# Sums of x ranked behind weight pieces, and first evictions by ScalarE or VectorE, in an attention and mixture-of-experts kernel

## The chip, the cores and the metric

The kernel runs on one core of one Trainium2 chip. The metric is the time of one execution on the device in microseconds (us), the median of several runs. Lower is better. The core's engines are TensorE (PE; PEld is its weight load), VectorE (DVE), ScalarE (ACT), GpSimd (POOL) and SyncE (SP), which issues most transfers. Each engine takes its instructions in the order in which the program lists them.

## The reference

Causal attention with a cumulative decay, then a soft mixture of four experts, then a gated network, all in f32:

```python
cum = np.cumsum(np.maximum(s, 0), axis=-1)
scores = q @ k.T / sqrt(64) + np.minimum(-(cum[:, None] - cum[None, :]), 0)   # causal; 2 x 8 heads, 576 x 64
x = softmax(scores) @ v                                  # heads side by side: x is 1152 x 512
p = domain_probs / domain_probs.sum(-1)                  # 1152 x 4
x = sum(p[:, e:e+1] * (np.maximum(x @ w1[e], 0) @ w2[e]) for e in range(4))    # 512 -> 1024 -> 512
g = x @ w_gate                                           # 512 -> 1536
out = (g / (1 + np.exp(-g)) * (x @ w_val)) @ w_out       # 1152 x 512
```

## The kernel before

**Numbers in two parts.** Every dense operand is split into a high part, rounded to TensorE's f32 format, and a low part, the rest. A product takes three matmuls (high by high, high by low, low by high). Names end accordingly: xh and xl for x, wah and wal for weights that lead in, woh and wol for weights that lead out, hh and hl for the hidden values, wsh and wsl for sums of weights. A high part is a cast, a low part a subtraction.

**Seven products for eight.** Where it pays, a product x @ w is cut in quarters and done with seven products instead of eight, which needs sums of quarters of w (`Weight.halves`, tile sf, line 930) and sums of quarters of x (`sums_of_x`, tile tt, line 1097). A sum of x is some additions and subtractions of two operands in SBUF, then a cast (line 307) and a low part (line 320). The seven results are added up in the tile cc by VectorE straight out of the banks (lines 1177 and 1198).

**Stages.** The 1152 tokens go in two parts, 0 to 512 (four tiles of 128 tokens) and 512 to 1152 (five tiles). A stage leads one part of the tokens through 256 hidden columns. Its matmuls in (tile h) alternate with the matmuls out (tile o) of the stage before. A tile of output is six matmuls into one bank of PSUM, called o. Then it is evicted: `moe1_out` multiplies it by the expert's share p and writes it into acc_a (first part) or acc_b (second part) the first time (line 1302), and adds it to what is there every later time (line 1304). `moe2_out` copies the first time (line 1447) and adds later (line 1449). All evictions are on VectorE. There are three o banks in the dense part, so a tile waits until the tile three before it has been evicted.

**The order.** The program plans itself while it is written. Every task has an engine or a choice of engines with a cost each, the tasks it depends on, and a rank. At each step the task with the earliest start goes next, and among equal starts the one with the lowest rank. A task with a choice takes the engine for which start plus 1.6 times the cost is least, with 1.0 us on top for VectorE in the dense part. Evictions and what else TensorE soon waits for have the rank `prompt()`, 69 at the end of attention. Weight pieces (casts and low parts of a weight, in two pieces each) have 100 plus the number of the weight, and 11 weights are planned by then. The sums of x for the first part had the rank 70, thus behind evictions and ahead of all weight pieces; those for the second part had 109. They are planned when attention ends, near 145 us. The chosen order is fixed in the program: on the chip an engine waits for the next instruction in its list even if a later one could run.

In `COST` a sum of two operands (kind "two") of 256 columns is put at 0.48 us on VectorE and 0.81 us on GpSimd, a read of a bank (kind "bank") of 512 columns at 0.61 us on VectorE and 0.48 us on ScalarE.

Of the kernel before, what the change touches and what calls it, by code (L numbers as in the profile page):

```python
# [55 lines left out]
WRANK = 100  # L56
# [28 lines left out]
def f32(ap):  # L85
    return ap.bitcast(F32)
# [13 lines left out]
def dve(c, n=1):  # L100
    return n * 0.07 + 0.00105 * c
# [11 lines left out]
def choices(engines, kind, c, n=1):  # L113

    return {e: n * COST[kind][e][0] + c * COST[kind][e][1] for e in engines}
# [38 lines left out]
class Plan:  # L154
# [8 lines left out]
    def add(self, eng, cost, run=None, deps=(), take=(), give=(), rank=0.0):  # L163
        t = Task(eng, cost, run, [d for d in deps if d is not None], take, give, rank)
        if not t.missing:
            self.ready.append(t)
        return t
# [96 lines left out]
def attention_moe_swiglu(ctx, tc, q, k, v, s, dp, w1, w2, wg, wv, wo, out):  # L264
    nc = tc.nc
    B, H, S, D = q.shape
    N, DM = out.shape
# [26 lines left out]
    late = {}  # L294
    plan = Plan()
    add = plan.add
    rings = {}

    def ring(name, n=2):
        return rings.setdefault(name, Ring(n))  # L300

    def any_of(engines, kind, c, run, deps, n=1, **kw):
        return add(choices(engines, kind, c, n), None, run, deps, **kw)

    def move(e, to, x):
        if e == "a":
            nc.scalar.copy(to, x)  # L307
        elif e == "v":
            nc.vector.tensor_copy(to, x)
        else:  # L310
            nc.gpsimd.tensor_scalar(to, f32(x), 1.0, 1.0, op0=ALU.mult, op1=ALU.mult)
# [7 lines left out]
    def minus(e, to, x, y):  # L319
        {"v": nc.vector, "p": nc.gpsimd}[e].tensor_tensor(to, x, f32(y), op=ALU.subtract)  # L320
# [10 lines left out]
    def pieces():  # L331

        for (tok, n), pos in zip(runs, place):
            a = 0
            while a < n:
                t, p = divmod(pos + a, P)
                m = min(P - p, n - a)
                yield t, slice(p, p + m), slice(tok + a, tok + a + m)
                a += m
# [636 lines left out]
    def acc(t):  # L976
        if t < HALF // P:
            return acc_a[:, t, :]
        return late["acc"][:, t - HALF // P, :]
# [15 lines left out]
    made = {"n": 0}  # L995
# [40 lines left out]
    def prompt():  # L1036
        return newest["i"] - DRANK

    def needs_x(t0, t1):
        if t0 in x_ready:  # L1040
            return x_ready[t0]
        return [x for g in range(len(groups)) if place[g] < t1 for x in done_x[g]]
# [31 lines left out]
    def sums_of_x(t0):  # L1074

        n = (N - HALF if t0 else HALF) // 2
        box = late["T", t0]

        deps = needs_x(t0, t0 + 2 * n) + late.get("sums", [])
        done = box["done"] = {}  # L1080

        def quarter(x, i, j, c):
            return f32(x[:, 2 * i + c, t0 + j * n:t0 + j * n + n])
        tmp = {}
        rg = ring("tt")

        rank = WRANK + made["n"] - 2 if t0 else prompt() + 1
        SUB, ADD = ALU.subtract, ALU.add

        def total(name, x, y, op, deps, new=False):  # L1090

            def task(c, at):
                def run(on):
                    if new and c == 0:
                        tmp[name] = late["t"].tile([P, 6 * P], F32, name="tt", tag="tt", bufs=2)[:, :2 * n].rearrange("p (c n) -> p c n", c=2)
                    x_, y_ = (tmp[z][:, c] if isinstance(z, str) else quarter(*z, c) for z in (x, y))
                    {"v": nc.vector, "p": nc.gpsimd}[on].tensor_tensor(tmp[name][:, c], x_, y_, op=op)
                return any_of(TADD, "two", n, run, at, take=[rg] if new and c == 0 else [], rank=rank)
            first = task(0, deps[0])
            return [first, task(1, deps[1] + ([first] if new else []))]  # L1100

        def chain(*lists):
            return [[x[c] for x in lists] for c in range(2)]

        def parts(i, name, t):
            done[i] = []
            for c in range(2):
                def high(on, c=c):
                    move(on, box["h"][:, i, c], tmp[name][:, c])

                def low(on, c=c):
                    minus(on, box["l"][:, i, c], tmp[name][:, c], box["h"][:, i, c])
                hi = any_of(THIGH, "copy", n, high, [t[c]], rank=rank)
                done[i].append(any_of(TLOW, "two", n, low, [hi], rank=rank))
            return done[i]
        a1 = total("T1", (xh, 0, 1), (xh, 0, 0), SUB, [deps, deps], True)
        t = total("T1", "T1", (xl, 0, 1), ADD, chain(a1))
        t1 = total("T1", "T1", (xl, 0, 0), SUB, chain(t))
        a2 = total("T2", (xh, 1, 1), "T1", SUB, chain(t1), True)
        t2 = total("T2", "T2", (xl, 1, 1), ADD, chain(a2))  # L1120
        u2 = parts(1, "T2", t2)
        u1 = parts(0, "T1", t1)

        t = total("T1", "T2", (xh, 0, 0), SUB, chain(u1, t2))
        t3 = total("T1", "T1", (xl, 0, 0), SUB, chain(t))
        u3 = parts(2, "T1", t3)
        add(None, 0.0, None, u3, give=[(a1[0], rg)])
        t = total("T2", (xh, 1, 0), "T2", SUB, chain(u2, t3))
        u4 = parts(3, "T2", total("T2", "T2", (xl, 1, 0), ADD, chain(t)))
        add(None, 0.0, None, u4, give=[(a2[0], rg)])  # L1130
        late["sums"] = [x for y in done.values() for x in y]
# [73 lines left out]
    def order(st):  # L1205

        return [t for t in ORDER if st.t0 <= t * P < st.t1]
# [32 lines left out]
    fresh = set(range(NT))  # L1240
    last_acc = {}
# [51 lines left out]
    def moe1_out(w, st, e):  # L1293
        items = []

        for t in order(st):
            def evac(x, taker, bank_, t=t):
                def run():
                    sc = pr[:, t, e:e + 1]
                    if t in fresh:  # L1300
                        fresh.remove(t)
                        nc.vector.tensor_scalar(acc(t), bank_(), sc, None, op0=ALU.mult)
                    else:
                        nc.vector.scalar_tensor_tensor(acc(t), bank_(), sc, acc(t), op0=ALU.mult, op1=ALU.add)  # L1304
                a = add("dve", 0.74, run, [x, last_acc.get(t), late["gates"]], give=[(taker, ring("o"))], rank=prompt())
                last_acc[t] = a
                left[t] -= 1
                if left[t] == 0:
                    turn_x(t, a)
            items += outof(w, st, t, evac)  # L1310
        return items
# [129 lines left out]
    def moe2_out(w, st, first, last):  # L1441
        items = []
        for t in order(st):
            def evac(x, taker, bank_, t=t):
                def run():
                    if first:
                        nc.vector.tensor_copy(acc(t), bank_())  # L1447
                    else:
                        nc.vector.tensor_tensor(acc(t), bank_(), acc(t), op=ALU.add)
                deps = [x, last_acc.get(t)] + (turning[st.t0]["turned"] if first else [])  # L1450
                a = add("dve", dve(DM), run, deps, give=[(taker, ring("o"))], rank=prompt())
                last_acc[t] = a
                if last:
                    for p, tok in [y[1:] for y in pieces() if y[0] == t]:
                        add("dma", (0.65, 0.37) if p.stop - p.start < P else (0.48, 0.73), lambda p=p, tok=tok: nc.sync.dma_start(out[tok, :], acc(t)[p, :]), [a], rank=0)
            items += outof(w, st, t, evac)
        return items
# [124 lines left out]
    with ExitStack() as st:  # L1582
        late["ps"] = st.enter_context(tc.tile_pool(name="psb", bufs=1, space=PSUM, reuse_waits="tile"))
        late["t"] = st.enter_context(tc.tile_pool(name="tm", bufs=2, reuse_waits="tile"))
        late["h"] = late["t"]
        late["acc"] = late["t"].tile([P, NT - HALF // P, DM], F32, name="acc_b", bufs=1)
        for t0, n in ((0, HALF), (HALF, N - HALF)):
            late["T", t0] = {x: late["t"].tile([P, 4, 2, n // 2], F32R, name=f"x{x}{t0}", bufs=1) for x in "hl"}
            sums_of_x(t0)
        late["made_n"] = 0  # L1590
        plan.held = HELD2
        rings["h"].n, rings["o"].n = 5, 3
        feed()
        while plan.step():
            feed()
# [24 lines left out]
```

## Time and profile before

| | us |
|---|---|
| median of 3 runs | 749.46 (749.1 to 751.05) |
| profiled execution | 744.91 |
| its span, first to last instruction | 743.1 |
| TensorE busy in it | 717.8 (97%) |
| VectorE busy | 626.6 (84%) |
| GpSimd busy | 440.2 (59%) |
| ScalarE busy | 362.8 (49%) |

The span is attention up to about 143 us (with dense work filling in from 39 us on), the mixture of experts up to about 528 us, and the gated network. TensorE's granted clock is full all the time. A busy share is a mean over parts with different limits, so the places at which TensorE waits, and what runs on the other engines there, tell more than the shares. The times in the rows are us from the start of the span; "idle before" stands in square brackets, with the instruction that ended it.

### The profile page before, as it was taken

How to read it: one execution, taken by the hardware profiler on the slowest of the kernel's cores; microseconds unless marked ns; L12 is line 12 of the kernel's file. 1: busy time of each engine (PE TensorE's matmuls, PEld its weight loads, DVE VectorE, ACT ScalarE, POOL GpSimd, SP SyncE). 2: the span in 40 equal slices, each digit the busy share in tenths (PEclk: the TensorE clock that was granted, in tenths of full speed). 3: DMA queues.
4: the chain of work that ended last, by engine and by line, in shares of the span. 5: the costliest groups of instructions: out<-in, count | busy, mean ns of one | idle time of the engine just before them, and what ended most of it. 6: DMA issues, size and time to landing. Idle time of an engine off the chain costs nothing. (4 is left out here: it accounts for less than half of the span.)

```text
span 743.1 us, 12433 instructions
## 1 busy us (share of the span) xinstructions
PE 717.8 (97%) x4328; PEld 625.4 (84%) x4328; DVE 626.6 (84%) x1273; ACT 362.8 (49%) x808; POOL 440.2 (59%) x456
## 2 busy tenths in 40 slices
PE   8899999998999999999999999998989999999997
PEld 6577776767889989898998989897888999999996
DVE  7979888599678998989999899898997888787765
ACT  6788767324234546455564554574641423232210
POOL 6546865389336456454555455778885676765321
PEclk9999999999999999999999999999999999999999
DMA  5657630010314524444344543622110101010003
GB/s 130 139 119 201 158 90 30 1 56 30 121 49 143 180 82 165 144 168 143 105 165 141 184 156 105 204 90 99 58 57 29 58 30 57 29 58 1 1 1 127
DMA packets 77230, 72.57 MB, mean 98 GB/s; under 512 B 45976, under 2 KB 56280, under 8 KB 77168
## 3 DMA queue, kind: packets, MB, share of 16 engines
q1 hardware_dynamic: 76112, 71.52, 31.3%
q8 instruction: 34, 0.56, 0.3%
q10 hardware_dynamic: 1056, 0.26, 0.2%
q14 instruction: 28, 0.23, 0.1%
HBM read 59.82 MB, written 11.80 MB: 96 GB/s over the span
## 5 line engine op out<-in xcount | busy, mean ns | idle before, releaser
L1220 PE MATMUL o<-woh,hh 128*128 128x512 f32 x396 | 156.5, 395 | 3.6 <-DVE acc_a L1304 2.0
L1221 PE MATMUL o<-wol,hh 128*128 128x512 f32 x396 | 156.1, 394 | 1.7 <-POOL wol L320 1.7
L1222 PE MATMUL o<-woh,hl 128*128 128x512 f32 x396 | 154.8, 391 | 2.2 <-DVE hl L320 2.2
L1177 DVE TENSOR_TENSOR cc<-cc,h 128x320 f32<-128x320 f32 (+1 forms) x288 | 127.7, 451 | 30.6 <-PE h L1160 26.1
L320 POOL TENSOR_TENSOR wal<-raw,wah 128x512 fp32r<-128x512 f32 (+1 forms) x56 | 68.6, 1236 | 71.4 <-ACT wah L307 70.9
L1158 PE MATMUL h<-xh,wsh 128*128 128x320 f32 (+1 forms) x320 | 95.0, 297 | 0.0
L1160 PE MATMUL h<-xh,wsl 128*128 128x320 f32 (+1 forms) x320 | 95.0, 297 | 0.0
L1159 PE MATMUL h<-xl,wsh 128*128 128x320 f32 (+1 forms) x320 | 94.9, 297 | 0.0
L1222 PEld LDWEIGHTS o<-woh,hl 128*128 128x128 f32 x396 | 74.4, 188 | 19.4 <-DVE hl L320 3.0
L1220 PEld LDWEIGHTS o<-woh,hh 128*128 128x128 f32 x396 | 74.5, 188 | 17.4 <-DVE acc_a L1304 2.5
L1221 PEld LDWEIGHTS o<-wol,hh 128*128 128x128 f32 x396 | 74.5, 188 | 13.2 <-POOL wol L320 2.4
L320 POOL TENSOR_TENSOR wol<-raw,woh 128x512 fp32r<-128x512 f32 x52 | 74.4, 1443 | 15.4 <-ACT woh L307 15.2
L1277 ACT ACTIVATE cc<-cc 128x640 f32<-128x640 f32 (+1 forms) x48 | 33.4, 695 | 93.1 <-DVE cc L1177 93.1
L1158 PE MATMUL h<-xh,wah 128*128 128x256 f32 (+1 forms) x240 | 71.3, 297 | 0.0
L1160 PE MATMUL h<-xh,wal 128*128 128x256 f32 (+1 forms) x240 | 71.1, 296 | 0.0
L1159 PE MATMUL h<-xl,wah 128*128 128x256 f32 (+1 forms) x240 | 71.0, 296 | 0.0
L320 POOL TENSOR_TENSOR hl<-cc,hh 128x512 fp32r<-128x512 f32 (+1 forms) x24 | 33.1, 1379 | 50.4 <-DVE hl L823 24.9
L1158 PEld LDWEIGHTS h<-xh,wsh 128*128 128x128 f32 x320 | 60.4, 189 | 1.6
L1159 PEld LDWEIGHTS h<-xl,wsh 128*128 128x128 f32 x320 | 60.5, 189 | 1.4
L1160 PEld LDWEIGHTS h<-xh,wsl 128*128 128x128 f32 x320 | 60.5, 189 | 0.0
L1304 DVE SCALAR_TENSOR_TENSOR acc_b<-o,pr,acc_b 128x512 f32<-128x512 f32 x75 | 55.8, 746 | 4.8 <-PE o L1222 4.1
L307 ACT CAST hh<-sg 128x512 fp32r<-128x512 f32 (+1 forms) x24 | 16.2, 676 | 85.7 <-DVE sg L1421 43.2
(155 smaller groups left out, 1835.1 us busy)
## 6 DMA issues: line engine op xcount, KB each, us to landing
raw<-in_moe_w SPq DMA_DIRECT2D x40, 512.0 KB
n<-hl SPq DMA_DIRECT2D x36, 256.0 KB
raw<-n SPq DMA_DIRECT2D x18, 512.0 KB
hh<-in_moe_w_gate SPq DMA_DIRECT2D x12, 512.0 KB
hh<-in_moe_w_val SPq DMA_DIRECT2D x12, 512.0 KB
hh<-in_moe_w_out SPq DMA_DIRECT2D x12, 512.0 KB
kr<-in_k SPq DMA_DIRECT2D x24, 128.0 KB
vr<-in_v SPq DMA_DIRECT2D x24, 128.0 KB
```

Source lines behind the costliest of these rows:

```text
L307: nc.scalar.copy(to, x)
L320: {"v": nc.vector, "p": nc.gpsimd}[e].tensor_tensor(to, x, f32(y), op=ALU.subtract)
L1158: nc.tensor.matmul(hp, wh, h, start=c == 0, stop=False)
L1159: nc.tensor.matmul(hp, wh, l, start=False, stop=False)
L1160: nc.tensor.matmul(hp, wl, h, start=False, stop=c == 1)
L1177: nc.vector.tensor_tensor(part(k), part(x), banks[i], op=ALU.add)
L1220: nc.tensor.matmul(op, hh[:, f, ts], wh[:, f, :], start=f == 0, stop=False)
L1221: nc.tensor.matmul(op, hh[:, f, ts], wl[:, f, :], start=False, stop=False)
L1222: nc.tensor.matmul(op, hl[:, f, ts], wh[:, f, :], start=False, stop=f == NF - 1)
L1277: nc.scalar.activation(src()[:, o], src()[:, o], AF.Relu)
L1304: nc.vector.scalar_tensor_tensor(acc(t), bank_(), sc, acc(t), op0=ALU.mult, op1=ALU.add)
```

## The change

Three edits. In `sums_of_x` the rank of the sums of the first part becomes 109 (from 70), and that of the second part 111 (from 109). The first eviction of each tile in `moe1_out` (nine in all) and in `moe2_out` (nine) gets a choice between ScalarE and VectorE, at the cost of a bank read; later evictions stay on VectorE. The words for the change also name score operands that are not filled with zeros; the instructions that fill score operands are the same in both programs.

```diff
-        rank = WRANK + made["n"] - 2 if t0 else prompt() + 1
+        rank = WRANK + made["n"] - (0 if t0 else 2)
...
-                def run():
+                new = t in fresh
+                fresh.discard(t)
+
+                def run(on="v"):
                     sc = pr[:, t, e:e + 1]
-                    if t in fresh:
-                        fresh.remove(t)
+                    if on == "a":
+                        nc.scalar.mul(acc(t), bank_(), sc)
+                    elif new:
                         nc.vector.tensor_scalar(acc(t), bank_(), sc, None, op0=ALU.mult)
...
-                a = add("dve", 0.74, run, [x, last_acc.get(t), late["gates"]], give=[(taker, ring("o"))], rank=prompt())
+
+                a = add(choices("av", "bank", DM) if new else "dve", None if new else 0.74, run,
+                        [x, last_acc.get(t), late["gates"]], give=[(taker, ring("o"))], rank=prompt())
...
-                def run():
+                def run(on="v"):
                     if first:
-                        nc.vector.tensor_copy(acc(t), bank_())
+                        move(on, acc(t), bank_())
...
-                a = add("dve", dve(DM), run, deps, give=[(taker, ring("o"))], rank=prompt())
+                a = add(choices("av", "bank", DM) if first else "dve", None if first else dve(DM), run, deps, give=[(taker, ring("o"))], rank=prompt())
```

On GpSimd, behind the four pieces of wah and wal that run from 144.31 us on in the trace of before, there stood (tt is a sum of x, xl_2260 its low part, woh and wol are pieces of an out-weight):

```order
L1097 TENSOR_TENSOR tt<-tt,xl 128x256
L320 TENSOR_TENSOR xl_2260<-tt,xh_2259 128x256 x2
L1097 TENSOR_TENSOR tt<-tt,xl 128x256
L1097 TENSOR_TENSOR tt<-tt,xh 128x256
L320 TENSOR_TENSOR xl_2260<-tt,xh_2259 128x256
L1097 TENSOR_TENSOR tt<-tt,xl 128x256
L311 TENSOR_SCALAR woh<-raw 128x512
L1097 TENSOR_TENSOR tt<-xh,tt 128x256
L320 TENSOR_TENSOR xl_2260<-tt,xh_2259 128x256 x2
L1097 TENSOR_TENSOR tt<-tt,xl 128x256
L320 TENSOR_TENSOR wol<-raw,woh 128x512
```

and now, on the same engine at the same place:

```order
L311 TENSOR_SCALAR woh<-raw 128x512
L1097 TENSOR_TENSOR tt<-xh,tt 128x256
L320 TENSOR_TENSOR wol<-raw,woh 128x512
L311 TENSOR_SCALAR woh<-raw 128x512
L320 TENSOR_TENSOR xl_2260<-tt,xh_2259 128x256
L320 TENSOR_TENSOR wol<-raw,woh 128x512
L1097 TENSOR_TENSOR tt<-tt,xh 128x256
L1097 TENSOR_TENSOR tt<-tt,xl 128x256
L1097 TENSOR_TENSOR tt<-xh,tt 128x256
L311 TENSOR_SCALAR woh<-raw 128x512
```

The first wol piece moved from the twelfth instruction and later to the third; four of the five low parts of sums that stood here left for VectorE.

On VectorE, ahead of the eviction of the first tile of the out stage that begins at 160.97 us in the trace (the last row here), there stood:

```order
L1097 TENSOR_TENSOR tt<-xh,tt 128x256
L1302 TENSOR_SCALAR acc_a<-o,pr 128x512
L1097 TENSOR_TENSOR tt<-tt,xl 128x256
L1302 TENSOR_SCALAR acc_a<-o,pr 128x512
L320 TENSOR_TENSOR xl_2260<-tt,xh_2259 128x256 x2
L1097 TENSOR_TENSOR tt<-xh 128x320
L1261 SCALAR_TENSOR_TENSOR hl<-h,hh 128x512
L1097 TENSOR_TENSOR tt<-xh 128x320
L1097 TENSOR_TENSOR tt<-tt,xl 128x320 x4
L1304 SCALAR_TENSOR_TENSOR acc_a<-o,pr,acc_a 128x512
```

and now (line 1308 is what was 1304):

```order
L1097 TENSOR_TENSOR tt<-xh,tt 128x256
L320 TENSOR_TENSOR xl_2260<-tt,xh_2259 128x256
L1097 TENSOR_TENSOR tt<-tt,xl 128x256
L320 TENSOR_TENSOR xl_2260<-tt,xh_2259 128x256 x3
L1097 TENSOR_TENSOR tt<-xh 128x320
L1261 SCALAR_TENSOR_TENSOR hl<-h,hh 128x512
L1097 TENSOR_TENSOR tt<-xh 128x320
L1097 TENSOR_TENSOR tt<-tt,xl 128x320 x2
L1308 SCALAR_TENSOR_TENSOR acc_a<-o,pr,acc_a 128x512
```

The two first evictions left for ScalarE, low parts of sums came in, and two of the four additions of the next sums moved behind the eviction.

On VectorE in the first stage of the gated network, from 549.86 us on in the trace (hl<-sf is the low part of a weight sum, hl<-sg one of a hidden value, sg the gated value), there stood:

```order
L320 TENSOR_TENSOR hl<-sf,hl 128x512
L1447 COPY acc_a<-o 128x512
L320 TENSOR_TENSOR hl<-sf,hl 128x512
L1177 TENSOR_TENSOR cc<-cc,h 128x320
L1447 COPY acc_a<-o 128x512
L1421 TENSOR_TENSOR sg<-sg,cc 128x640
L1198 TENSOR_TENSOR cc<-cc,h 128x320
L1447 COPY acc_a<-o 128x512
L1177 TENSOR_TENSOR cc<-cc,h 128x320
L1421 TENSOR_TENSOR sg<-sg,cc 128x640
L1447 COPY acc_a<-o 128x512
```

and now (line 1427 is what was 1421):

```order
L320 TENSOR_TENSOR hl<-sf,hl 128x512 x2
L1177 TENSOR_TENSOR cc<-cc,h 128x320
L1427 TENSOR_TENSOR sg<-sg,cc 128x640
L1198 TENSOR_TENSOR cc<-cc,h 128x320
L320 TENSOR_TENSOR hl<-sg,hh 128x640
L1177 TENSOR_TENSOR cc<-cc,h 128x320
L1427 TENSOR_TENSOR sg<-sg,cc 128x640
L320 TENSOR_TENSOR wsl<-sf,wsh 128x512
L1177 TENSOR_TENSOR cc<-cc,h 128x256
L320 TENSOR_TENSOR hl<-sg,hh 128x640
```

The four copies left for ScalarE; two low parts hl<-sg came in from GpSimd, and behind these rows a low part wsl and two weight sums sf went to GpSimd.

## Rows read from the trace of the kernel before

**Rows 1.** Waits of TensorE over the run: waiter, releaser: us in total, times, longest

```profile
PE h L1158 <- DVE cc L1177: 2.7, 3, 1.9
...
PE o L1220 <- DVE acc_a L1304: 2.0, 1, 2.0
PE o L1221 <- POOL wol L320: 1.7, 1, 1.7
...
PE h L1158 <- DVE cc L1198: 0.8, 1, 0.8
```

**Rows 2.** Timeline of TensorE, 160.9 to 184.2 us: start, duration, engine, line, instruction

```profile
164.25 0.50 PE L1221 MATMUL o<-wol,hh 128*128 128x512 f32 x1 [1.71 <-POOL wol L320]
...
168.98 0.39 PE L1220 MATMUL o<-woh,hh 128*128 128x512 f32 x1
169.20 0.39 PE L1221 MATMUL o<-wol,hh 128*128 128x512 f32 x1
...
183.77 0.50 PE L1220 MATMUL o<-woh,hh 128*128 128x512 f32 x1 [2.04 <-DVE acc_a L1304]
```

**Rows 3.** Busy by stretch: stretch, length, PE, PEld, DVE, ACT, POOL, clock, DMA

```profile
147.50:183.70 36.20, 32.49 (x155) 26.60 (x154) 36.13 (x50) 12.27 (x28) 33.22 (x34) 1.00 0.14 44
549.90:565.20 15.30, 13.72 (x88) 12.18 (x87) 15.11 (x24) 4.57 (x9) 13.42 (x12) 1.00 0.18 65
184.00:469.00 285.00, 285.00 (x1655) 256.35 (x1654) 248.87 (x401) 144.78 (x256) 146.90 (x130) 1.00 0.43 140
```

**Rows 4.** Groups by shape, 147.5 to 183.7 us: count, busy us, mean ns, idle before

```profile
L1304 DVE SCALAR_TENSOR_TENSOR acc_a<-o,pr,acc_a 128x512 f32<-128x512 f32 x7 | 5.2, 740 | 0.0
...
L1261 DVE SCALAR_TENSOR_TENSOR hl<-h,hh 128x512 fp32r<-128x512 f32 x4 | 2.7, 678 | 0.0
...
L1302 DVE TENSOR_SCALAR acc_a<-o,pr 128x512 f32<-128x512 f32 x2 | 1.5, 739 | 0.0
L1261 DVE SCALAR_TENSOR_TENSOR hl<-h,hh 128x320 fp32r<-128x320 f32 x3 | 1.4, 477 | 0.0
```

**Rows 5.** Timeline of VectorE, 143 to 203 us

```profile
147.18 0.41 DVE L1097 TENSOR_TENSOR tt<-xh 128x256 f32<-128x256 f32 x1
147.51 2.73 DVE L1097 TENSOR_TENSOR tt<-tt,xl 128x256 f32<-128x256 f32 x3
...
167.59 0.74 DVE L1304 SCALAR_TENSOR_TENSOR acc_a<-o,pr,acc_a 128x512 f32<-128x512 f32 x1
...
182.98 0.74 DVE L1304 SCALAR_TENSOR_TENSOR acc_a<-o,pr,acc_a 128x512 f32<-128x512 f32 x1
```

**Rows 6.** Timeline of GpSimd, 143 to 203 us

```profile
159.04 0.92 POOL L1097 TENSOR_TENSOR tt<-tt,xl 128x256 f32<-128x256 f32 x1
159.92 1.30 POOL L320 TENSOR_TENSOR wol<-raw,woh 128x512 fp32r<-128x512 f32 x1
...
162.70 3.00 POOL L320 TENSOR_TENSOR wol<-raw,woh 128x512 fp32r<-128x512 f32 x2
```

**Rows 7.** Timeline of TensorE, three pieces between 561.6 and 565.5 us

```profile
562.04 0.38 PE L1158 MATMUL h<-xh,hh 128*128 128x256 f32 x1 [0.36 <-DVE cc L1177]
...
563.46 0.39 PE L1158 MATMUL h<-xh,hh 128*128 128x256 f32 x1 [0.46 <-DVE cc L1177]
...
565.27 0.39 PE L1158 MATMUL h<-xh,hl 128*128 128x256 f32 x1 [0.84 <-DVE cc L1198]
```

**Rows 8.** Groups by shape on VectorE, 549.9 to 565.2 us

```profile
L1447 DVE COPY acc_a<-o 128x512 f32<-128x512 f32 x4 | 2.7, 685 | 0.1
...
L320 DVE TENSOR_TENSOR wsl<-sf,wsh 128x512 fp32r<-128x512 f32 x2 | 2.4, 1199 | 0.0
L320 DVE TENSOR_TENSOR hl<-sf,hl 128x512 fp32r<-128x512 f32 x2 | 2.2, 1110 | 0.0
L930 DVE TENSOR_TENSOR sf<-raw 128x256 f32<-128x256 f32 x2 | 1.7, 866 | 0.0
```

**Rows 9.** Timeline of ScalarE near 108 us, a copy out of a bank

```profile
107.87 0.56 ACT L307 COPY p<-tp 128x512 f32<-128x512 f32 x1
```

## The prediction

> **What bounds the kernel now.** I read the waits of TensorE first. TensorE is busy nearly all the time, and in the long middle stretch from 184 to 469 us it is never idle: 285.00 of 285.00 us [rows 3]. So only the places where it waits can give time back. Of these the change touches three. Near 164 us it waits for a low weight part on GpSimd, near 184 us for the copy of an output tile out of its bank on VectorE, and near 562 to 565 us for VectorE additions into cc [rows 1]. The reader is to see in each row who came last.
>
> In the timeline of TensorE the first is 1.71 us of idle before the matmul at 164.25, the second 2.04 us before the one at 183.77 [rows 2]; the last are 0.36, 0.46 and 0.84 us [rows 7]. A stop costs a little more than the idle shown: a matmul is drawn 0.39 us long, but the next starts 0.22 us behind it [rows 2], so each stop adds some 0.15 us, and the five cost about 1.9, 2.2 and together 2.1 us: 6.2 us of the span of 743.1. Of the 2.7 us for cc [rows 1], 1.9 lie at 545 us, ahead of everything that the change reorders there; they stay.
>
> Then I asked what VectorE does there. From 147.5 to 183.7 us it is busy 36.13 of 36.20 us, from 549.9 to 565.2 us 15.11 of 15.30 [rows 3]. GpSimd is busy 33.22 of 36.20 us in the first stretch. So both engines are full where TensorE waits, and moving work from one to the other is not free.
>
> **The first stretch, 147.5 to 184 us.** The change ranks the sums of x behind most weight pieces. In the order on GpSimd, the pieces of the next out-weight now come before most sums. In the run before they ended with two pieces from 162.70 on, 3.00 us long [rows 6], and TensorE at 164.25 waited for the first of them. In the new order two high and two low pieces stand in the first six rows behind the pieces of wah, with one sum and one low part between. At 1.3 us for a low piece [rows 6], 0.8 for a high piece and 0.9 for a sum they are done some 7 us after 149 us, thus by 157 us, against a need at 161 us. This wait goes.
>
> What is late next is VectorE. Its list gets more sums, since the cost table sends a sum to whichever engine looks free, and GpSimd now has weight pieces. I count the rows of its order from 147.5 us up to the release that TensorE needs at 183.77 (the first of the two evictions of acc_a with 'x2' shown, the seventh of that kind in both orders). Before: 30 instructions on sums, 2 weight sums, 7 evictions into acc_a, 2 first evictions, 4 and 3 low parts out of a bank. After: 35 on sums, no weight sum, the same 7, 4 and 3, and no first eviction. What reads a bank takes 5.2 + 2.7 + 1.4 us and, before, 1.5 us for the two first evictions [rows 4], less 0.07 us each for the overlap with the next (0.41 us drawn from 147.18 on, next start 147.51 [rows 5]): 8.3 us now, 9.6 before. The rest before, 36.2 - 9.6 = 26.6 us, is 32 instructions with two operands in SBUF, 0.83 us each. So the release falls at 147.5 + 8.3 + 35 m, with m the mean of a sum.
>
> For m there are two bounds. Left alone, a sum of 256 columns starts its follower 0.33 us later; beside GpSimd three took 2.73 us, 0.91 each [rows 5]. The low end m = 0.41 (as the row of 147.18) puts the release at 170 us: VectorE then no longer decides, and both waits go, 4.1 us. At the old mean, m = 0.83, it falls at 184.9 us against the end of the eviction at 182.98 + 0.74 = 183.72 [rows 5]: 1.1 us later than before, and the gain at 164 us is all handed back and more. In between decides what a sum waits for. The rows look like turns taken: a sum on GpSimd takes 0.92 us beside VectorE [rows 6], about 0.58 of its own and 0.34 of waiting. If the two go one after the other, the stretch loses 5 sums on GpSimd (5 x 0.58 = 2.9 us) and gains 3 two-operand instructions on VectorE (3 x 0.34 = 1.0 us); the weight pieces up to that point are as many as before. That is 1.9 us less: 24.7 us for 35, m = 0.71; and if the 1.3 us of the first evictions ran beside GpSimd anyway, their going gives nothing, and m is 0.74 in effect. I take the later: the release 1.9 us earlier, at 181.8 us. TensorE would be there in time: with the wait at 164 us gone it could start the fourth tile of the first out stage (168.98 [rows 2]) as early as 167.1; the release that this tile needs ended at 167.59 + 0.74 = 168.33 [rows 5], and by the same sum (22 sums at 0.74 and 3.8 us of bank reads) ends at 167.6. From there to the point at 183.77 it has 12.6 us of matmuls, so it arrives at 180.3 and waits 1.5. **Term 1: -1.9 us**, between -4.1 and +1.1. So most of what is gained at 164 us is waited out at 184 us, and the wait there gets shorter, not gone.
>
> The Trainium skill (SBUF — State Buffer, Who interferes with whom) says that a VectorE instruction with two SBUF inputs and a GpSimd instruction that reads SBUF exclude each other for the whole instruction, and that one with at most one SBUF input doesn't. The trace agrees with the first half: 0.41 us alone against 0.91 beside GpSimd. Taken strictly it speaks against this change, as each sum moved to VectorE can wait out a whole weight piece instead of another sum; that is the slower rival below.
>
> The evictions into acc_b (191 to 198 us) now run on ScalarE. A copy of 512 columns out of a bank takes 0.56 us there [rows 9], TensorE has no idle behind them in the run before [rows 3], and VectorE idles around them: 0.
>
> **The second stretch, 549.9 to 566 us.** The nine first evictions of the last network go to ScalarE; four of them, 2.7 us less 0.3 for overlap, stood here on VectorE [rows 8]. Its list also loses one of two low parts of a weight sum (1.2 us) and two weight sums (1.7 us) to GpSimd, and gets two low parts of 640 columns. Their like with 512 columns took 1.11 us [rows 8], so 1.39 each, 2.8 us; an end from the 1.20 us of wsl is 3.0. Net: 2.4 + 1.2 + 1.7 - 2.8 = 2.5 us less by the time of the last wait at 565.27, and 2.4 + 1.2 - 2.8 = 0.8 less at the first one at 562.04, where the weight sums don't yet count. Asked for are 0.5 us at the first and 2.1 us at the last. **Term 2: -2.1 us**, as nothing more than the waits can be won; at the dearer end it still covers the last wait and half a microsecond of the first. If ScalarE, which takes its copies in order and now waits for output tiles, holds up a cast, the term shrinks to 0 at worst; ScalarE is busy 4.57 of 15.30 us here [rows 3], so I take none of it.
>
> **The attention stretch, 104 to 147 us.** One of two first evictions (0.74 us, as in [rows 4]) moves to ScalarE at 0.56 us [rows 9], and a dozen small items change engines or places. TensorE's small waits there have different releasers, ScalarE among them. **Term 3: 0**, from -0.7 to +0.7, the price of one eviction either way. The PE order changes by a few neighbours only; I count that at 0. DMA issues keep their order, so no queue moves.
>
> **Sum.** -1.9 - 2.1 + 0 = -4.0 us. The profiled run has 744.91 us for a span of 743.1; it would have 740.9. The median of the three timed runs is 749.46, 4.5 us above the profiled one; the same work is saved, so 745.5 us.
>
> **Rivals.**
> - Both waits of the first stretch go: VectorE is left alone more than I think (m at or below 0.68, the release by 179.7 us, when TensorE comes). Then -4.1 - 2.1 = -6.2: 743.3 us. For it: five sums fewer on GpSimd, and the serial count gave 0.71. Against: GpSimd is nearly full until 170 us in the new order too.
> - The first stretch gives nothing: m stays at 0.83, +1.1 - 2.1 = -1.0: 748.5 us. For it: it is the measured mean, and weight pieces are longer than sums.
> - Slower: sums wait behind weight pieces. In the new order weight pieces of 1.3 to 1.5 us [rows 6] stand between the sums; a sum that waits out one takes about 1.5 us instead of 0.9. If 10 of the 35 meet one more often than before, the stretch grows by 6 us over m = 0.83's share: m = 1.0, release at 190.8, +7.1 - 2.1 = +5.0: 754.5 us. It turns slower by more than 0.3% (2.2 us) from m = 0.92 on. Against it: the number of weight pieces up to there is the same as before.
> - The change doesn't do what it says: the freed VectorE time near 562 us is lost to waits on GpSimd or ScalarE, and the first stretch breaks even: 749.5 us.
>
> **How the numbers follow.** The forecast has 0.46, both waits gone 0.18, nothing in the first stretch 0.20, no effect at all 0.06, slower 0.10. A measurement of this kernel can tell about 0.3%, 2.2 us, from no change. Forecast and both-gone are faster: 0.64. The two next are within: 0.26. Slower: 0.10. The range runs from the first rival with term 3 at its end, 743.3 - 0.7 and some 0.4 for the spread of the median, to the third case with the same, 748.5 + 0.7 + 0.4, and on toward the slower one until about 2 in 10 are outside: 742.2 to 750.4.
>
> **What would show it.** Right: no TensorE wait for wol near 162 us; one for the eviction near 182 us, about 1.5 us long; none for cc between 555 and 564 us while the one near 544 us keeps 1.9 us; the sums on VectorE at a mean near 0.74 us. Wrong: a wait for an eviction near 168 us that was not there, a mean above 0.83 us, ScalarE rows near 550 us that start late behind a copy, or any new wait in the middle stretch.

## The result and the profile after

The changed kernel takes 741.43 us (median of 10 runs, 740.29 to 743.21). In the first comparison it was 742.11 against 749.38 us, a ratio of 0.9898 (95% interval 0.9876 to 0.9921); in a second one, among the experiments, 741.19 against 746.63, 0.9911 (0.9878 to 0.9943; the two medians alone give 0.9927). The forecast was 745.5, the range 742.2 to 750.4: right in sign, 3.4 to 4.1 us too careful, and outside the range by 0.1 us in the first comparison and by 0.8 over all 10 runs.

| | before | after | after, again |
|---|---|---|---|
| profiled execution, us | 744.91 | 741.40 | 740.51 |
| its span, us | 743.1 | 739.5 | 738.6 |
| mean granted clock of TensorE in it | 1.000 | 0.992 | 1.000 |

The profile after has the second span. Its waits of TensorE (waiter, releaser: us in total, times, longest), which answer to [rows 1]:

```profile
PE o L1220 <- DVE acc_a L1308: 2.3, 1, 2.3
...
PE h L1158 <- DVE cc L1177: 1.9, 1, 1.9
```

The wait for wol is gone, the three waits for cc near 562 us are gone, and the one of 1.9 us that stayed is where the prediction left it. But the eviction that TensorE waits for (line 1308 is what was 1304) is another one. The timeline of TensorE, which answers to [rows 2]:

```profile
164.39 0.39 PE L1222 MATMUL o<-woh,hl 128*128 128x512 f32 x1
167.06 0.50 PE L1220 MATMUL o<-woh,hh 128*128 128x512 f32 x1 [2.28 <-DVE acc_a L1308]
167.39 0.46 PE L1221 MATMUL o<-wol,hh 128*128 128x512 f32 x1
167.65 0.63 PE L1222 MATMUL o<-woh,hl 128*128 128x512 f32 x1
168.08 0.63 PE L1220 MATMUL o<-woh,hh 128*128 128x512 f32 x1
...
181.32 0.39 PE L1220 MATMUL o<-woh,hh 128*128 128x512 f32 x1
...
543.24 0.42 PE L1158 MATMUL h<-xh,hh 128*128 128x320 f32 x1 [1.91 <-DVE cc L1177]
```

The stop is now at the fourth tile of the first out stage (167.06 is the matmul that stood at 168.98 in [rows 2]); at 181.32, once the place of a 2.04 us wait, TensorE goes on without one. In the second profile of after the stop is 2.58 us long, and at the old place a wait of 0.59 us is left:

```profile
167.09 0.50 PE L1220 MATMUL o<-woh,hh 128*128 128x512 f32 x1 [2.58 <-DVE acc_a L1308]
...
180.57 0.50 PE L1220 MATMUL o<-woh,hh 128*128 128x512 f32 x1 [0.59 <-DVE acc_a L1308]
```

In the first profile, behind the stop, a matmul of 512 columns starts 0.43 us after the one before, where it was 0.23. The busy time by stretch says why (length, then PE, PEld, DVE, ACT, POOL, then the granted clock):

```profile
167.60:171.00 3.40, 3.40 (x12) 2.96 (x11) 3.40 (x7) 2.56 (x6) 2.90 (x3) 0.50 0.27 61
171.10:183.70 12.60, 12.60 (x72) 11.37 (x71) 12.47 (x20) 4.92 (x13) 10.48 (x11) 1.00 0.20 65
546.00:562.00 16.00, 16.00 (x109) 14.98 (x109) 14.77 (x23) 8.62 (x17) 15.08 (x14) 1.00 0.27 88
```

From 167.6 to 171.0 us TensorE's clock was at 1.2 GHz, the lower of its two levels. The last row is the second stretch of [rows 3], shifted: TensorE is never idle in it.

To see where the time went I take each matmul's start in one timeline from that of the same matmul in the kernel before (negative: earlier). Since the profile of before has full clock throughout, the second profile of after, which has it too, is the one to compare:

| at (before's time) | after | after, full clock |
|---|---|---|
| 104.2 us, attention | +0.14 | -0.13 |
| 128.7 | -1.89 | -2.16 |
| 164.8, past the old wait for wol | -4.35 | -4.62 |
| 169.7, past the new stop | -1.58 | -1.76 |
| 183.8, past the old wait for acc_a | -2.46 | -3.21 |
| 545.6 | -2.39 | -3.27 |
| 565.7, past the waits for cc | -4.78 | -5.69 |
| 738.5, the last out stage | -4.78 | -5.69 |
| end of the span | -3.6 | -4.5 |

Three things were not in the prediction: 2.2 us gained in the attention, 1.2 us lost at the very end, and a clock that isn't the same in every run.

### The profile page after: what moved, and what is told of

It is laid out like the page before. It is cut to its first block, busy times and chain, and to the rows that moved or that the text cites. A ratio compares the mean times of both kernels' runs of the same rounds, so it can differ in the third digit from the quotient of the medians.

```text
span 739.5 us, 12436 instructions
## 1 busy us (share of the span) xinstructions
PE 720.2 (97%) x4328; PEld 629.9 (85%) x4328; DVE 612.2 (83%) x1255; ACT 372.2 (50%) x829; POOL 440.0 (60%) x453
## 4 chain that ended last, share of the span: by engine, by line
PE 76%; DVE 11%; ACT 5%; POOL 4%; issue 3%; DMA 1%; POOLq 0%; DVEq 0%; ACTq 0%
PE o L1220 11%; PE h L1158 11%; PE o L1222 11%; PE h L1160 11%; PE o L1221 11%; PE h L1159 11%; PE sp L621 2%; DVE ns L630 2%; DVE tt L1097 2%; PE tp L667 1%; ACT ns L637 1%; PE h L1058 1%; PE h L1060 1%; PE h L1059 1%; PE po L717 1%
## 5 line engine op out<-in xcount | busy, mean ns | idle before, releaser
L1308 DVE SCALAR_TENSOR_TENSOR acc_a<-o,pr,acc_a 128x512 f32<-128x512 f32 x60 | 44.5, 744 | 12.2 <-PE o L1222 11.8
```

## Experiments on the clock

**The kernel before, again.** No edit.

> The kernel before, unchanged, to see its clock in timed runs. Theory clock: the profiled run of before had full clock throughout, while its timed runs, 4.5 us longer, had stretches at 1.2 GHz behind waits, as the profiled run of after has three (behind 20.8, 167.6 and 515.7 us). Then timed runs show a granted clock near 0.985 to 0.99 and 748 to 751 us, and a profile with full clock, if it comes, some 745. Rival offset: timed runs are 4.5 us longer for a reason outside the span (launch, transfers), with a clock of 1.00 in runs of 749 us.

Measured: median 747.52 us (744.70 to 750.39) at clocks of 0.988 to 1.000, so lower and wider than either theory had it. Each run has its own mean clock, and the time follows it. Over 72 runs of the kernel before, this one's among them (one more, of 2460.92 us, is left out), the mean is 744.9 us at a clock of 0.997 and more (14 runs), 746.9 at 0.994 to 0.996 (18), 748.3 at 0.990 to 0.993 (24) and 750.3 below that (16). So 744.91 us, the profiled run with 1.000, is simply the kernel at full clock, and the 4.5 us to the median are no fixed addition. In this run's profile one such stretch stands behind the wait for cc (start, duration; the wait in brackets):

```profile
548.44 0.42 PE L1158 MATMUL h<-xh,hh 128*128 128x320 f32 x1 [1.91 <-DVE cc L1177]
548.69 0.31 PE L1159 MATMUL h<-xl,hh 128*128 128x320 f32 x1
548.84 0.31 PE L1160 MATMUL h<-xh,hh 128*128 128x320 f32 x1
...
549.13 0.45 PE L1159 MATMUL h<-xl,hh 128*128 128x320 f32 x1
549.37 0.47 PE L1160 MATMUL h<-xh,hh 128*128 128x320 f32 x1
549.64 0.47 PE L1158 MATMUL h<-xh,wsh 128*128 128x320 f32 x1
```

A matmul of 320 columns starts its follower 0.15 us later at first (548.69) and 0.24 to 0.27 us later from 549.13 on. In the profile of [rows 1] the same wait had full clock behind it.

**The changed kernel, again.** No edit.

> The changed kernel, unchanged, beside the others of this set. In its profiled run three stretches of 3.4 us had half the clock (from 20.8, 167.6 and 515.7 us) and its granted clock was 0.992. Theory clock (the time follows how many such stretches a run has): single runs spread over 4 us or more, those at a clock of 0.998 or more near 739 us, those at 0.992 near 741.5, those at 0.988 near 743. Theory offset (timed runs lie a fixed 4.5 us above a profiled one, as before): all runs within 1 us of one another near 742 to 746, whatever their clock.

Measured: 740.5 and 740.9 us at a clock of 1.000, 740.3 at 0.998, 741.5 to 742.4 at 0.994 and 0.995. The offset theory falls here too, though the spread is 2.1 us and not the 4 that I had expected, and full clock gives 740.5 and not 739. At 0.997 and more the two kernels are 740.6 and 744.9 us, 4.3 apart. At their medians they are 6.1 apart (741.43 against 747.53), since the mean clock of the changed kernel's 10 runs is 0.9957 and that of the 72 is 0.9928.

**Stops where there are none.** In the kernel before, VectorE fills a scratch tile ahead of four evictions of the middle stretch:

```diff
+                    nth[0] += 1
+                    if nth[0] in (40, 58, 76, 94):
...
+                        for _ in range(30):
+                            nc.vector.memset(late["stop"], 0.0)
```

> The kernel before with 30 fills of 128 x 128 on VectorE ahead of four evictions, near 253, 300, 347 and 394 us, where TensorE is never idle in the kernel before. Each holds up VectorE by some 4 us, and TensorE has to wait 1 to 2.5 us for a bank some three tiles later. Theory clock (a stop of TensorE of that size is often followed by 3.4 us at half clock, which cost 1.7 us more): in the profile half-clock stretches stand behind some of the four stops and nowhere else between 200 and 460 us, the granted clock of the runs is lower than that of the kernel before (0.98 to 0.995), and the time is 6 to 14 us above it, more than the idle time alone. Theory clock by itself (the half-clock stretches come at times that have nothing to do with stops): none or any number of stretches between 200 and 460 us, not behind the stops; the time is longer by the idle time alone, 4 to 9 us.

Measured: 777.26 us, 1.040 of before (1.034 to 1.046), 29 us more where I had expected 6 to 14. I had put a fill too low (the 30 took 7.66 us at the first, not 4), so each stop is 4.7 to 4.9 us. The first, in the timeline of TensorE, and then by stretch the time ahead of it and the first two stops:

```profile
255.99 0.31 PE L1160 MATMUL h<-xh,wal 128*128 128x320 f32 x1
261.03 0.80 PE L1220 MATMUL o<-woh,hh 128*128 128x512 f32 x1 [4.73 <-DVE acc_a L1312]
261.62 0.63 PE L1221 MATMUL o<-wol,hh 128*128 128x512 f32 x1
...
268.03 0.40 PE L1220 MATMUL o<-woh,hh 128*128 128x512 f32 x1
```

```profile
200.00:255.00 55.00, 55.00 (x321) 49.71 (x321) 42.88 (x77) 23.72 (x44) 25.36 (x22) 1.00 0.31 104
258.40:265.40 7.00, 4.37 (x14) 3.80 (x15) 6.05 (x16) 0.81 (x2) 0.21 (x1) 0.51 0.31 122
313.00:320.00 7.00, 4.72 (x16) 4.15 (x17) 5.86 (x15) 1.15 (x3) 0.00 (x0) 0.51 0.26 98
```

The clock falls while TensorE is idle, at all four stops, and nowhere else between 200 and 460 us. It comes back 4.3 us after work has resumed at the first and 4.6 to 5.0 at the others. The stops set TensorE back by 7.0 to 7.4 us each (29.0 behind the fourth): 4.7 to 4.9 idle, and 2.2 to 2.5 behind, nearly all of it the low clock. So these stops cost half as much again as their idle time. Behind the shorter stops of the two kernels and of the runs below, 1.5 to 2.6 us, the clock fell in some executions and not in others (not behind the 2.58 us at the same place in the full-clock profile of after). Where it fell, a short stop cost relatively more: some 1.5 us on top of 2.0 and 2.1 in two of the runs below. Why it falls in one and not in the other stays open.

## Experiments on the parts

**The ranks alone.** In the kernel before:

```diff
-        rank = WRANK + made["n"] - 2 if t0 else prompt() + 1
+        rank = WRANK + made["n"] - (0 if t0 else 2)
```

> Only the ranks of the sums of x change; first evictions stay on VectorE. Theory waits (each edit gives the idle it takes away where it stands): the wait for wol at 164 us goes (-1.9), a wait for the eviction near 168 us comes instead and is longer than the 2.3 us of after, since two first evictions (1.3 us) are back on VectorE; -0.5 to +1 us in all, 749 to 750.5. Attention unchanged in time up to 145 us. Theory clock: one wait of over 2 us instead of two, so one stretch at 1.2 GHz less (1.7 us): 746.5 to 748.

Measured: 746.96 against 747.51 us, 0.9985 (0.996 to 1.0009): no change that can be told. At a clock of 0.997 and more it is 744.0 to 744.7 (four runs) against 744.9. The one wait of TensorE between 140 and 200 us:

```profile
PE o L1220 <- DVE acc_a L1304: 2.1, 1, 2.1
```

The wait for wol goes, and TensorE gains 2.5 us on the kernel before; it gives 2.4 back at the fourth tile and 1.5 more to the low clock behind that stop; the old wait at 183.77 is then gone, 2.2 us. Left are 0.7. Alone, the ranks swap two stops for one that costs nearly as much. I had expected that stop to be longer than the 2.3 us of after; it is 2.1.

**The first evictions of `moe1_out` alone**, the second part of the diff.

> Only the first evictions of the experts may run on ScalarE. Theory waits: attention ends 1.9 us earlier as in after; the wait for wol near 162 us stays at 1.7 us of idle, the one for the eviction near 182 us shrinks by up to the 1.3 us of two first evictions; -2 to -3.2 us, 746 to 747.5. Theory clock: the same or up to 1.7 us more, 744.5 to 747.5.

Measured: 743.71 us, 0.9957 (0.9931 to 0.9982). In its profile TensorE is 2.1 us ahead by 128.7 us and 2.6 ahead from 165 us to the middle; its waits for wol and for acc_a stay, 1.7 and 2.0 us. I had expected the second to shrink by up to 1.3 us; it didn't.

**The first evictions of tiles 0 and 1 alone**, which stand in the attention: the same edit with `new and t < 2` for `new`.

> The kernel before, and only the first evictions of tiles 0 and 1, which stand in the attention, may go to ScalarE (one of them does). Theory relief (the 1.9 us that the changed kernel gains between 104 and 128 us come from VectorE having one eviction less there): TensorE is 1.9 us earlier than in the kernel before from 128 us on, and the time is 1.5 to 2.2 us lower at equal clock. Theory elsewhere (they come from the ranks or other evictions): no shift at 128 us, and the time of the kernel before within 0.5 us at equal clock.

Measured: 743.95 us, 0.9966 (0.9945 to 0.9986); at a clock of 0.997 and more 742.9 to 743.3, 1.8 below the kernel before. From 104.2 to 128.7 us TensorE gains 2.0 us. The waits of TensorE between 100 and 130 us, in the kernel before and then here:

```profile
PE tp L667 <- ACT p L307: 0.8, 1, 0.8
PE sp L621 <- DVE st L630: 0.8, 2, 0.4
```

```profile
PE tp L667 <- POOL ns L317: 0.2, 1, 0.2
PE tp L667 <- ACT p L307: 0.2, 1, 0.2
```

The two waits for st (line 630, where VectorE reads the scores out of their banks) go, and most of the wait behind them. The relief theory stands in the main: VectorE has less to do there. But it isn't the eviction alone. The plan is made anew around it, and up to 130 us five copies and casts of other tiles go to ScalarE too, while one copy comes back and one scaling comes from GpSimd. The changed kernel moves the same items, so the 2 us belong to the edit with all that it drags along; what the eviction is worth by itself no run shows.

**The first evictions of `moe2_out` alone**, the last part of the diff.

> Only the first evictions of the gated network may run on ScalarE. Theory waits: the three waits for cc between 562 and 565 us go, -2.1 us, all else the same: 747.3. Theory clock: if a stretch at 1.2 GHz follows the waits at 545 to 565 us in timed runs of before, up to 1.7 us more: 745.5 to 747.3.

Measured: 745.54 us, 0.9969 (0.9948 to 0.9991). Two of the three waits for cc go and 0.2 us of the last is left; TensorE gains 2.0 us between 561 and 566 us.

**Both first evictions, no ranks.** The changed kernel with the first part of the diff undone.

> The changed kernel with the rank edit undone: both edits on first evictions, none on ranks. 22 sums instead of 24 stand on VectorE before the eviction of the first tile of the out stage at 161 us. Theory ranks pay (they take away the wait for wol at 164 us, 1.9 us, and the second wait is bounded by VectorE): the wait for wol is back with 1.7 us idle, and the time is 1 to 2 us above that of the changed kernel at equal clock. Theory ranks swap one wait for another (what is gained at 164 us is waited out at 167 us): the time at equal clock is the changed kernel's within 0.7 us, about 739 us with full clock, and the wait at 167 us is gone or below 0.5 us.

Measured: 742.24 us against 741.19 for the changed kernel beside it; at a clock of 0.995 742.3 (three runs) against 741.9 (two). Its waits between 140 and 200 us are both back, the second at 181.76:

```profile
PE o L1220 <- DVE acc_a L1308: 2.0, 1, 2.0
PE o L1221 <- POOL wol L320: 1.6, 1, 1.6
```

3.6 us of stops here, 3.2 (2.58 and 0.59) in the changed kernel at full clock: most of what the ranks gained, VectorE's list took. I had expected the wait at 167 us to be gone or below 0.5 us, and it is gone; the one that comes back at 181.76 I had not named. The times understate the ranks a little: at the end of the program SyncE waits 1.6 us here and 2.8 in the changed kernel, for a reason of its own (the experiment on the end), so up to there the ranks are worth 1.2 us more than the 0.4 at equal clock.

## Experiments on the first stretch

**A cost of their own for the sums.** In the changed kernel, for the planning alone:

```diff
+    "sum": {"v": (0.35, 0.0015), "p": (0.247, 0.0026)},
...
-                return any_of(TADD, "two", n, run, at, take=[rg] if new and c == 0 else [], rank=rank)
+                return any_of(TADD, "sum", n, run, at, take=[rg] if new and c == 0 else [], rank=rank)
...
-                done[i].append(any_of(TLOW, "two", n, low, [hi], rank=rank))
+                done[i].append(any_of(TLOW, "sum", n, low, [hi], rank=rank))
```

> The changed kernel, but a sum of x is given a cost of its own in the planner's table (0.73 us on VectorE and 0.91 on GpSimd for 256 columns, about what the trace shows, in place of 0.48 and 0.81), for the planning alone. 15 sums instead of 24 then stand on VectorE before the eviction that TensorE waited for at 167.06 us (2.28 us idle). Theory queue (that wait is VectorE's list of sums): the wait near 167 us is gone or under 0.3 us, with it the half-clock stretch right behind it (1.7 us); the span at equal clock is 2 to 2.4 us shorter than that of the changed kernel, the median 2 to 4 us lower. Theory both full (GpSimd can't take the sums either): the first matmuls that need the sums, or weight pieces near 162 us, are late instead, and the time is the same within 1 us.

Measured: 737.58 us, 0.9858 of before (0.982 to 0.9897), 3.6 below the changed kernel beside it; 735.9 at a clock of 0.997 against 740.3 at 0.998. TensorE has no wait between 140 and 200 us:

```profile
147.50:181.00 33.50, 33.50 (x164) 28.52 (x163) 31.10 (x42) 12.75 (x27) 31.16 (x33) 1.00 0.26 79
```

The queue theory stands: the stop near 167 us was VectorE's list, and GpSimd had room for the sums. Not all of the gain is the queue's, though: the wait at the end of the program is 1.6 us here and 2.8 in the changed kernel, so 1.2 us of it lie there. It is the fastest version here, by 9 us over the kernel before beside it (746.63) and by 10 over the median of the 72.

**The same cost without the ranks.** The kernel above with the first part of the diff undone.

> The kernel with the sums' own cost (e5) and the rank edit undone: first evictions by ScalarE or VectorE, sums at their own cost, ranks as before. 17 sums instead of 15 stand on VectorE before the eviction that TensorE may wait for near 167 us. Theory ranks pay once VectorE has room: the wait for wol near 162 us is back, 1.6 us, and the time is 1.5 to 2.5 us above that of e5 at equal clock. Theory room alone pays (with VectorE's list shorter, GpSimd has the sums, and the pieces of wol are late in either order): the time is that of e5 within 0.7 us.

Measured: 747.32 us, 0.9986 of before (0.9964 to 1.0008), 9.7 above the one with the ranks; at a clock of 0.995 745.5 to 745.7 (three runs) against 737.2 (one), 8.4. The waits between 140 and 200 us:

```profile
PE h L1061 <- POOL wal L321: 3.2, 2, 2.0
PE o L1222 <- POOL wol L321: 2.4, 1, 2.4
```

Now GpSimd holds the sums ahead of the weight pieces, and three pieces come late. I had expected 1.5 to 2.5 us. So the ranks can't be told from nothing alone and are worth 8 to 10 us beside the new cost. The new cost gains 3.6 us with the ranks, 1.2 of them at the end, and without them loses 5.1 by the medians (742.24 above) and 3.3 at a clock of 0.995. The two pay together.

## An experiment on the end

At the end of the program SyncE waits for the last transfer of the output. Its wait in the kernel before, then in after, and a row of what the queues moved in the last 3.6 us of after, which has no like in before:

```profile
SPq L1616 <- DMA out<-acc_b: 1.6, 1, 1.6
```

```profile
SPq L1622 <- DMA out<-acc_b: 2.8, 1, 2.8
```

```profile
q14 instruction: 1, 0.01, 0.5%
```

A fetch of 8 KB of code (0.01 MB in the row; 28 such packets in the whole span are 0.23 MB) falls among the packets of the last transfer. VectorE has 18 instructions fewer than before (1255 for 1273 on the pages), so I suspected its next piece of code. The test adds eight tiny fills to its list, in the attention:

```diff
             sm = const.tile([P, NT], F32, name="sm")
+            for _ in range(8):
+                nc.vector.memset(sm, 0.0)
```

> The changed kernel with eight tiny fills (128 x 9) more on VectorE in the attention; the order on all engines is otherwise the same. In both profiles of the changed kernel 8 KB of code were fetched 2.55 us after the start of the last eviction, among the packets of the last output transfer, and the span ended 4.90 us after that start instead of 3.74 as before. Theory code fetch (VectorE's list is 18 instructions shorter than before, and the fetch of its next piece slid into the last transfer): with the longer list the fetch comes some 12 us before the last eviction, the span ends 3.74 us behind it, and the time at equal clock is 0.6 to 1.2 us lower than that of the changed kernel (the fills cost at most 0.5). Theory something else at the end (the last transfer itself, or the queue): 4.90 us stay, and the time is the same or up to 0.5 us higher.

Measured: 741.56 us. The fetch is 12.0 us ahead of the last eviction now, and the wait is as before:

```profile
SPq L1624 <- DMA out<-acc_b: 1.6, 1, 1.6
```

So 1.16 us at the end hang on where a fetch falls. The other traces agree: only the two profiles of the unaltered changed kernel have a fetch on q14 in their last 3.6 us, and only there the wait is 2.8 us. The median shows no gain. In the profiled execution TensorE is 2.1 us later by 128.7 us than in the first profile of after, with a longer stretch at 1.2 GHz near 20 us (6.8 us for 3.4); what of it is the fills isn't shown. At a clock of 0.995 the runs are 741.0 to 741.5 us (three) against 741.5 to 742.8 (three), too few to tell. The Trainium skill (Runtime: NRT & Kernel Launch, Instruction fetch mechanics) says that each engine's sequencer fetches the next block of its program over a queue of its own while it executes the current one, and that the cost is mostly hidden. The traces agree that such fetches have queues of their own (q8 and q14), and this one moved with VectorE's list; whether the others are hidden no run here measures. The blocks of this queue are 8 KB, not the 16 that it names.

## Why the prediction was wrong

**The sum of the schedule, -4.0 us, was nearly right:** at full clock the profiled execution went from 744.91 to 740.51, 4.4 us. But errors cancel in it: -2.2 (attention), -1.0 (first stretch), -2.4 (last network) and +1.2 (end).

**Term 3, the attention**, forecast 0 (at most 0.7 either way), was -2.2. I priced the eviction that moves, 0.74 us there and 0.56 on ScalarE (it takes 0.69, as it is a scaled copy), and took the small waits for a spread of causes. Two of them, 0.8 us, ended with VectorE, and what stood behind them in the chain of a softmax came earlier too; the run with this part of the edit alone gains it nearly all (2.0). The "dozen small items" that the prediction let go at nothing are part of it.

**Term 1, the first stretch**, forecast -1.9, was -1.0 at full clock (from a lead of 2.16 us to one of 3.18 behind it) and -0.6 in the first profile of after, with the low clock in it. The wait for wol went as told. What I had at 1.5 us near 182 us was none there, and 0.6 in the other profile. The step that failed is the release for the fourth tile: I had TensorE wait 0.5 us for it, and it waited 2.3 and 2.6, the sign that I had named as wrong. TensorE came about as worked out, at 164.8 (167.1 less the 1.9 us of lead is 165.2). The two evictions on VectorE in the profile after (start, duration):

```profile
166.26 0.74 DVE L1308 SCALAR_TENSOR_TENSOR acc_a<-o,pr,acc_a 128x512 f32<-128x512 f32 x1
...
179.72 1.40 DVE L1308 SCALAR_TENSOR_TENSOR acc_a<-o,pr,acc_a 128x512 f32<-128x512 f32 x2
```

The first ends at 167.00, 1.3 us later than my 167.6 less 1.9. By the sum of the prediction, shifted by the lead to 145.62, the 22 sums ahead of it took (167.00 - 145.62 - 3.8) / 22 = 0.80 us each. The second ends near 180.4, so all 35 took (180.4 - 145.62 - 8.3) / 35 = 0.76, against m = 0.74. The mean was nearly right for the stretch and wrong for its first part. By the same count the 19 instructions ahead of this eviction in the kernel before took 0.82 us each ((168.33 - 147.5 - 5.2) / 19, the 5.2 being the 3.8 and the two first evictions), so up to the fourth tile the mean had hardly fallen, and it fell behind it. Rows of VectorE and then of GpSimd in after show what kept it up:

```profile
158.59 1.51 DVE L1097 TENSOR_TENSOR tt<-tt,xl 128x256 f32<-128x256 f32 x1
...
162.96 1.58 DVE L1097 TENSOR_TENSOR tt<-xh 128x320 f32<-128x320 f32 x1
```

```profile
158.35 1.48 POOL L320 TENSOR_TENSOR wol<-raw,woh 128x512 fp32r<-128x512 f32 x1
...
162.72 1.47 POOL L320 TENSOR_TENSOR wal<-raw,wah 128x512 fp32r<-128x512 f32 x1
```

A sum that starts just behind a low weight piece ends only after the piece, having taken some 1.5 us instead of 0.4 to 0.9. Five of the 22 sums ahead of the eviction do so, where it was three of 19 before; of all 35 it is seven, where it was five of 32 (in the second profile of after six and eight). Two more at about 0.7 us above the 0.74 are about the 1.3 us by which the eviction was late. That is an estimate from these rows; no run takes the weight pieces away.

**Term 2, the last network**, forecast -2.1, was -2.4; it came as told, and each of the three restarts had cost some 0.1 us more than the 0.15 that I put.

**Not foreseen:** the 1.2 us at the end.

**The step that put the forecast outside** is the last one: "the same work is saved", so the median falls by what the profile falls. The profile of before was an execution at full clock; its median is one of executions with several stretches at 1.2 GHz, and most of those in the profiles stand behind a stop. At equal clock the kernels are 4.3 us apart; the rest, up to 6.1 at the medians over all runs, goes with the clock, 0.9928 against 0.9957. That the clock falls behind a stop is shown by the four made stops. That it is the removed stops that raise the mean clock is an inference, and a weak one: in the profile of before with a low clock (0.991) the stretches begin at 20.1, 166.9 and 549.1 us (6.8, 3.4 and 3.4 us long), and only the second stands behind a stop that the change takes away, while the first profile of after has one at 167.6, behind its new stop. With 10 runs of after the difference of the mean clocks may be partly chance.

The remaining 1.2 us, from 6.1 to the 7.3 of the first comparison, come with the draw of the runs: its medians lie 1.9 us (before) and 0.7 (after) above those over all runs. The 749.46 that the forecast started from is the median of three; all four timed runs of before in that comparison lie at 749.1 us or above, as 20 of the 72 do, and their clocks are not on record. From the median of the 72, 747.53, the same -4.0 would have given 743.5.

Of the rivals, "both waits go" (-6.2, 743.3 us) is the nearest to the medians, but by luck: at full clock the fall was 4.4, the second wait had moved and not gone, and the attention paid. The slower case, sums that wait out weight pieces, came in small: two more of them than before, against the ten that it supposed.

## What to carry to other kernels

Before a saving is taken off a median, see whether the profiled execution had the clock of the median's: a stop of TensorE can cost half as much again as its idle time or more, in some executions only, and a profile at full clock shows nothing of that. Where the median rests on three runs, take more before a forecast starts from it. Where work moves onto a full engine, time every release that TensorE needs along that engine's list, one after the other and with the durations of the instructions ahead of it, not only the one that waited before. Edits of an order are not additive: one can lose alone and gain beside another that takes away the stop it leaves, as the cost of the sums did without and with the ranks.

## What was not expected of the hardware

The clock of TensorE fell during each of four stops of 4.7 to 4.9 us, and returned 4.3 us after work began again at the first and up to 5.0 at the others; behind stops near 2 us it fell in some executions only. A fetch of 8 KB of code among the packets of the last transfer moved the end of the program by 1.16 us (2.8 us of waiting for 1.6), and eight more instructions on VectorE moved it back.
